# Operands of w2 that are raw blocks, the k chunks of turned heads, and who issues the copies

## The chip, the cores and the metric

One kernel runs on one core of a Trainium2 chip. Its time is the device time of one execution in microseconds (us), as the median of several executions; one further execution was profiled. Names used below: PE is TensorE (PEld its weight loads), DVE VectorE, ACT ScalarE, POOL GpSimd, SP SyncE. SP issues most transfers (DMAs), ACT some.

## The reference, cut to what matters

Two stages. A linear attention with decay gives x of 3072 tokens x 512; then four experts, each a product with w1, a relu and a product with w2, are summed with the tokens' gates.

```python
q, k, v: (4, 8, 768, 64); lam: (8,); w1: (4, 512, 1024); w2: (4, 1024, 512)
def _attn_ref(q, k, v, lam):
    for b in range(nb):                      # blocks of 64 tokens
        intra = np.einsum('bhic,bhjc->bhij', qb, kb) * Dmask[None]
        intra = np.einsum('bhij,bhjd->bhid', intra, vb)
        inter = np.einsum('bhid,bhde->bhie', qb * lam_pow[None], kv_state)
        out[:, :, sl] = intra + inter
        kb_dec = kb * rev_pow[None]
        kv_state = lam_block[None, :, None, None] * kv_state + np.einsum('bhsd,bhse->bhde', kb_dec, vb)
def _moe_ref(x, domain_probs, w1, w2):
    p = domain_probs / (domain_probs.sum(-1, keepdims=True) + 1e-09)
    for e in range(E):
        h = np.maximum(x @ w1[e], 0.0)
        out += p[:, e:e + 1] * (h @ w2[e])
```

## The kernel before

*Units.* The 3072 tokens are three groups of 1024, and a unit is a group g with an expert e: 12 units in the order (0; 0,1,2,3), (1; 1,2,3,0), (2; 2,3,0,1), so unit 5 is group 1 with expert 2, unit 7 group 1 with expert 0, and unit 11, FINAL, group 2 with expert 1. While the second product (with w2) of one unit runs on PE, the first product (with w1) of the next unit is interleaved with it, matmul group by matmul group.

*Products.* Every product is done by a scheme of 7 products of half-size blocks in place of 8, M1 to M7, the first product and from unit 5 on (NEST) the second product by two levels of it, the outer M and the inner M. The weights' side of outer product M is one of A11, A12, A22 (a raw block of the weight matrix) or S1 to S4 (a sum: S1 = A21 + A22, S2 = S1 - A11, S3 = A11 - A21, S4 = A12 - S2), by the table A_OF: M1 A11, M2 A12, M3 S4, M4 A22, M5 S1, M6 S2, M7 S3. Inside, the same table is applied to the quarters of that block, so that each outer product needs seven 128x256 operands: three raw quarters (A11, A12, A22) and four sums. The order of outer products in a unit is SEQ3 = M1, M3, M5, M7, M6, M2, M4; inner ones go in the order INNER = M1, M7, M6, M4, M5, M2, M3.

*Who makes the operands.* For w2 of each expert `prepare_w2_ops` lists steps ("chores"): load blocks of w2 into tiles w2b, form the outer sums w2o on POOL (`total`), and for each outer M form the four inner sums ops on POOL (`ready`, `inner_w2`) and store all seven operands to w_ops, that is w2_ops[e, M] in the chip's memory, 896 KB for one M. Later `feed3` loads them back in four transfers w2t (two operands of 128x256 at a time, the fourth one operand), or, for FINAL, in one transfer of all seven into a tile w2s that stays. `feed3` first calls `until(("w2", expert, M))`, which issues whatever chores and stores still stand ahead of that M, all at once.

*When they are issued.* The order of all instructions is fixed when the program is built. The loop at the end walks over units, outer products and 8 slots each; after each slot `pump` takes stores that are due and perhaps one chore from a list. Whether a chore is begun hangs on a planner's estimates: `busy` (POOL's work), `moved` (the transfer engines' work) and `asked` (SP's issues), of which the last two are raised by the helper `send` (L110 to L114) and compared with the slot now in `pump`. Transfers that a line issues by `dma_start` itself don't raise them. POOL and SP each go through their own list in order, and an instruction waits for what it needs, with all behind it on its engine.

*Attention of groups 1 and 2* runs in between, a chunk n of 128 tokens at a time (n = 8 to 23). `load` brings q and k in two transfers each, by r, the halves of the heads (h = 4r + i); the tile holds heads in the order i, r. `decayed` multiplies k by its decay on POOL. For chunks from 13 on (`comes_across`) q and k also come turned by another way: `bring_across` makes 128 small copies of q and k into a buffer `across`, issued by `trickle` one at a time: on SP, or on ACT where the argument says so, in unit 0's odd slots. `load_across` reads them.

*Lines for what follows.* L117 all POOL and DVE sums; L114 all transfers through `send`; L1148 PE, inner products of the first product; L1514 PE, inner products of the second product from unit 5 on; L1165 ACT relu of the first product's results, whose output m POOL multiplies with decay (m<-m,decay, the gates).

Of the kernel before, what the change touches and what calls it, by code (L numbers as in the profile page):

```python
# [12 lines left out]
ALU = mybir.AluOpType  # L13
# [8 lines left out]
def kernel(  # L22
# [30 lines left out]
    nc = tc.nc  # L53
# [38 lines left out]
    def small(name):  # L92
        return pool.tile([P, W], FP32, name=name, tag="t")
# [66 lines left out]
    def load(n, names="qkv"):  # L160

        c, b = where(n)
        for name in names:
            x = ({"k": acc_tile, "v": w2_tile} if n < CPG else {}).get(name, small)(f"{name}n")
            src = {"q": q, "k": k, "v": v}[name][b, :, c * C:(c + 1) * C, :]
            if name == "v":
                to, of = x[:].rearrange("p (h d) -> p h d", d=D), src.rearrange("h p d -> p h d")
                for h in (slice(0, 4), slice(4, 8)) if n < CPG else (slice(0, 8),):
                    send(out=to[:, h], in_=of[:, h], by=nc.scalar if n == 0 and h.start else None)
            else:  # L170
                to, of = x[:].rearrange("p (i r d) -> p i r d", r=2, d=D), src.rearrange("(r i) p d -> p i r d", r=2)
                for r in range(2):
                    by = nc.scalar if n == 0 and r == 1 else nc.sync
                    by.dma_start(out=to[:, :, r], in_=of[:, :, r])  # L174
            nat[n, name] = x[:].rearrange("p (h d) -> p h d", d=D)


# [15 lines left out]
    def store(f):  # L193
        queue.append((busy[0] + (8 if spare else 2), f))
# [125 lines left out]


    INNER = ("M1", "M7", "M6", "M4", "M5", "M2", "M3")

    def inner_w2(e, m, blk, two):
        b = {f"A{i + 1}{j + 1}": blk[j][:, :, i * P:(i + 1) * P] for i in range(2) for j in range(2)}
        s = [x.rearrange("p c d -> p (c d)").rearrange("p (k c d) -> p k c d", k=2, c=2) for x in two("ops")]
        for name, x, y, op in S_OPS:
            b[name] = s[SLOT[name] // 2][:, SLOT[name] % 2]
            tt(nc.gpsimd, b[name], b[x], b[y], op)
        to = w2_ops[e, MS.index(m)]  # L330
        b["S3"] = s[0]
        at = (("A11", 0), ("S3", slice(1, 3)), ("A22", 3), ("S1", 4), ("A12", 5), ("S4", 6))
        store(lambda: ([send(out=to[:, x], in_=b[n]) for n, x in at], made.add(("w2", e, m))))

    def prepare_w2_ops(e, eased):
        st = {}

        def two(name):
            if eased:
                t = [small(name)[:] for _ in range(2)]  # L340
            else:
                t = stage.tile([P, 2, W], FP32, name=name, tag="st")
                t = [t[:, q] for q in range(2)]
            return [x.rearrange("p (c d) -> p c d", c=2) for x in t]

        def block(name, i, j):
            t = st[name] = two("w2b")
            for q in range(2):
                r = j * W + q * 256
                src = moe_w2[e, r:r + 256, i * DH:(i + 1) * DH]  # L350
                send(out=t[q], in_=src.rearrange("(c p) d -> p c d", p=P))

        def total(name, a, b, op):
            t = two("w2o")
            for q in range(2):
                tt(nc.gpsimd, t[q], st[a][q], st[b][q], op)
            st[name] = t

        def ready(m):
            inner_w2(e, m, st[A_OF[m]], two)  # L360

        if not eased:
            return weight_steps(block, total, ready)

        def less():
            a, b = st["A11"], st.pop("A21")
            for q in range(2):
                tt(nc.gpsimd, b[q], a[q], b[q], ALU.subtract)
            st["S3"] = b

        def drop(*names):
            for n in names:
                del st[n]

        return [
            lambda: (block("A21", 1, 0), block("A22", 1, 1)), pause(6),
            lambda: total("S1", "A21", "A22", ALU.add),
            lambda: (ready("M4"), block("A11", 0, 0), drop("A22")), pause(4),
            less, lambda: ready("M7"), lambda: (ready("M1"), drop("S3")), lambda: ready("M5"),
            lambda: (total("S2", "S1", "A11", ALU.subtract), block("A12", 0, 1)), lambda: ready("M6"),  # L380
            lambda: ready("M2"),
            lambda: total("S4", "A12", "S2", ALU.subtract), lambda: ready("M3"),
        ]

# [272 lines left out]
    def decayed(n):  # L657

        kn = nat[n, "k"]
        kd = kn if n >= CPG else small("kd")[:].rearrange("p (h d) -> p h d", d=D)  # L660
        nat[n, "kd"] = kd
        by = k_decay.rearrange("p r ac -> p ac r").unsqueeze(3).to_broadcast([P, NHP, 2, D])
        tt(nc.gpsimd, *(x.rearrange("p (ac r) d -> p ac r d", r=2) for x in (kd, kn)), by, ALU.mult)

    carried = set()

# [20 lines left out]
    def turn(n, tags):  # L687
        all_added()
        begin_state(n)
        if comes_across(n):  # L690
            turn_across(n)
            return
        if n < CPG:
            decayed(n)
        qn, kn = nat.pop((n, "q")), nat[n, "k"]
        qp = bank(tags[0], "qp")
        kp = bank(tags[1], "kp")
        for x, y in ((qp, qn), (kp, kn)):
            for ac in range(NHP):
                nc.tensor.transpose(  # L700
                    out=x[:, ac * C:(ac + 1) * C], in_=y[:, 2 * ac:2 * ac + 2].rearrange("p r d -> p (r d)"),
                    identity=ident[:],
                )
        if n >= CPG:
            decayed(n)
        del nat[n, "k"]
        qT, kT = small("qT"), small("kT")
        nc.scalar.copy(out=qT[:], in_=qp[:])
        nc.scalar.copy(out=kT[:], in_=kp[:])
        if n >= CPG:  # L710
            turned[n] = qT, kT, qT
            return
        qs = small("qs")
        scaled = lambda: scale_q(qs, qp)
        soon(n, scaled)
        turned[n] = qT, kT, qs, scaled

    def scores(n, tags):
# [19 lines left out]
        for ac in range(NHP):  # L738
            for x in range(1 if last else 2):
                for r in range(2):  # L740
                    nc.tensor.matmul(  # L741
                        out=sp[x][half[r], 256 + ac * D:256 + (ac + 1) * D], lhsT=kd[half[x], 2 * ac + r],
                        rhs=vn[half[x], 4 * r + ac], start=False, stop=True, skip_group_check=True,
                    )
        st = small("st")
# [503 lines left out]
    def feed3(e, m, k):  # L1249

        x_e = units[e][1]
        until(("w2", x_e, m))
        if e == FINAL and m != SEQ3[0]:

            if k == 0:
                t = xp.tile([P, 7, 256], FP32, name="w2s", tag="x" + SEQ[SEQ3.index(m)])
                if (e, m) == PLAIN:
                    i, j = int(A_OF[m][1]) - 1, int(A_OF[m][2]) - 1
                    src = moe_w2[x_e, j * W:(j + 1) * W, i * DH:(i + 1) * DH]
                    send(out=t[:, 0:4], in_=src.rearrange("(k p) d -> p k d", p=P))  # L1260
                    fed3[e, m, 0] = t
                    return
                send(out=t[:], in_=w2_ops[x_e, MS.index(m)].rearrange("p k c d -> p k (c d)"))
                for x in range(4):
                    fed3[e, m, x] = t[:, 2 * x:min(2 * x + 2, 7)]
            return
        t = w2pool.tile([P, 2, DH], FP32, name="w2t", tag="w2")
        n = min(2, 7 - 2 * k)
        send(
            out=t[:, 0:n], in_=w2_ops[x_e, MS.index(m), :, 2 * k:2 * k + n].rearrange("p k c d -> p k (c d)"),  # L1270
        )
        fed3[e, m, k] = t

# [218 lines left out]
    def nested_product(e, m, tags):  # L1494
# [8 lines left out]

        def inner(x, i):
            if (e, m) == END and i in ("M2", "M3"):
                turned_product(("M2", "M3").index(i), b[B_OF[i]], fed3[e, m, x // 2][:, x % 2])
                return
            t = tags[0] if i in ("M1", "M6", "M5", "M3") else tags[1]
            fresh = i in ("M1", "M7", "M2")
# [2 lines left out]
            p = banks[t]  # L1512
            for c in range(2):
                nc.tensor.matmul(  # L1514
                    out=p[:, 0:256], lhsT=fed3[e, m, x // 2][:, x % 2, c * P:(c + 1) * P],
                    rhs=b[B_OF[i]][:, c * 256:(c + 1) * 256], start=(fresh and c == 0), stop=True,
                    skip_group_check=True,
                )
# [295 lines left out]
    for at, (g, e) in enumerate(units):  # L1814
# [14 lines left out]
        for i in range(7):  # L1829
# [41 lines left out]
            for x, part in enumerate(order):  # L1871
# [52 lines left out]
                while steps and (at * 7 + i) * 8 + x == steps[0][0]:  # L1924
                    steps.pop(0)[1]()
                if at == 0 or x % 2 or at == 1 and x == 4:
                    trickle(1, nc.scalar if at == 0 and x % 2 else None)
                for h in range(1, NG):
                    if x == 3 and 0 <= at * 7 + i - FILL[h] < 7:
                        x_fill(h, SEQ[at * 7 + i - FILL[h]])  # L1930
# [31 lines left out]
```

## Time and profile before

| | us |
|---|---|
| median of 3 runs | 1143.09 (1141.39 to 1143.7) |
| profiled execution, its own time | 1141.95 |
| its span, from the first to the last instruction | 1140.2 |
| PE busy | 1130.8 (7991 matmuls) |
| DVE, POOL, ACT busy | 771.7, 767.7, 381.1 |
| PE busy, 0 to 50 us | 44.38 of 50 |
| PE busy, 370 to 500 us | 130.00 of 130 |
| PE busy, 1090 to 1141 us | 46.83 of 51 |
| transfers: loads of w_ops for the second product, issues | 172 (129 of 256 KB, 43 of 128 KB) |
| transfers: stores of those operands, issues | 168 (28 of 256 KB, 140 of 128 KB) |

The profiled execution stands 1.14 us below the median of the runs. A line of a timeline gives the start, the time to the end of the group, engine, line, operation, output tile<-input tiles, shapes and how many there are; in square brackets stands the idle time of the engine before it and what ended it. Groups of transfers give their size and the median time from issue to landing. The granted clock (PEclk) is 1.00 in every stretch up to 1090 us and 0.98 in the last one.

### The profile page before, as it was taken

Reading aid. Unit: us, or ns where it says so; the run is one execution under the profiler, and the core shown is the slowest. Engines: PE = TensorE matmul, PEld = TensorE weight load, DVE = VectorE, ACT = ScalarE, POOL = GpSimd, SP = SyncE. Lnnn points to the kernel's source line nnn. Section 1 sums busy time; section 2 is a strip of 40 time slices with the busy share of each in tenths; the row PEclk is TensorE's granted clock in tenths of the full one; section 3 lists DMA queues with packets and bytes.
Section 4 is the critical chain, followed back from the end, with each engine's and each line's share of the span. In section 5 each row is a group of like instructions: output and inputs, shape, how many; then the busy total and the mean of one; then the engine's idle time right before and its main releaser. Section 6 shows DMA issues by size and latency. Waiting matters only on the chain.

```text
span 1140.2 us, 22167 instructions
## 1 busy us (share of the span) xinstructions
PE 1130.8 (99%) x7991; PEld 987.7 (87%) x7991; DVE 771.7 (68%) x1472; ACT 381.1 (33%) x770; POOL 767.7 (67%) x734
## 2 busy tenths in 40 slices
PE   8999999999999999999999999999999999999998
PEld 7788888888888888888888888888888888888887
DVE  4576775588577757837655566878767576776785
ACT  4325123212312321232343442444354452342332
POOL 2747148655852984854884997995995873873885
PEclk9999999999999999999999999999999999999999
DMA  8796889899989999987867669976779757657553
GB/s 195 173 281 183 214 226 265 276 299 279 310 270 323 301 311 303 312 279 233 260 204 249 200 182 286 347 241 199 223 235 277 217 161 213 189 159 214 168 194 74
DMA packets 321436, 271.58 MB, mean 238 GB/s; under 512 B 150640, under 2 KB 256304, under 8 KB 321328
## 3 DMA queue, kind: packets, MB, share of 16 engines
q1 hardware_dynamic: 298528, 264.37, 76.1%
q10 hardware_dynamic: 22768, 5.80, 2.5%
q8 instruction: 64, 1.05, 0.4%
q14 instruction: 44, 0.36, 0.1%
q0 software_dynamic: 32, 0.00, 0.0%
HBM read 197.19 MB, written 78.68 MB: 242 GB/s over the span
## 4 chain that ended last, share of the span: by engine, by line
PE 97%; SPq 1%; DMA 1%; DVE 0%; issue 0%; ACT 0%; DVEq 0%
PE pg L1148 41%; PE pq L1514 25%; PE q L1207 21%; PE pM L1656 2%; PE pc L1656 2%; PE op L797 1%; PE sp L734 1%; PE op L815 1%; PE sp L741 1%; DMA qn<-in_q_dram 1%; SPq L114 1%; PE pM L1381 1%; PE pg L1514 1%; SPq L174 0%; PE qp L700 0%; PE kp L700 0%
## 5 line engine op out<-in xcount | busy, mean ns | idle before, releaser
L1148 PE MATMUL pg<-xs,ws_in 128*128 128x256 f32 x1960 | 470.2, 380 | 0.4 <-DVE m L117 0.4
L1148 PEld LDWEIGHTS pg<-xs,ws_in 128*128 128x128 f32 x1960 | 371.0, 190 | 53.5 <-DVE m L117 3.2
L117 DVE TENSOR_TENSOR m<-pg,m 128x512 f32<-128x512 f32 x374 | 255.4, 686 | 91.7 <-PE pg L1148 81.4
L1207 PE MATMUL q<-w2t,m 128*128 128x256 f32 x1120 | 265.6, 380 | 0.0
L1207 PEld LDWEIGHTS q<-w2t,m 128*128 128x128 f32 x1120 | 211.7, 190 | 29.3 <-issue 0.3
L117 DVE TENSOR_TENSOR sums<-pq,sums 128x256 f32<-128x256 f32 x272 | 113.1, 421 | 90.6 <-PE pq L1514 78.4
L117 POOL TENSOR_TENSOR m<-m,decay 128x512 f32<-128x512 f32 x91 | 114.5, 1271 | 82.4 <-ACT m L1165 65.4
L1514 PE MATMUL pq<-acc,w2t 128*128 128x256 f32 x688 | 169.2, 379 | 0.0
L1514 PEld LDWEIGHTS pq<-acc,w2t 128*128 128x128 f32 x688 | 130.5, 190 | 18.0
L1165 ACT ACTIVATE m<-m 128x512 f32<-128x512 f32 x99 | 62.4, 630 | 190.9 <-DVE m L117 186.7
L1225 DVE SCALAR_TENSOR_TENSOR acc<-q,gate,acc 128x256 f32<-128x256 f32 x108 | 52.0, 482 | 75.6 <-PE q L1207 74.8
L117 DVE TENSOR_TENSOR m<-m,m 128x512 f32<-128x512 f32 x108 | 96.6, 894 | 6.5 <-ACT m L1131 6.5
L1161 ACT COPY m<-pg 128x512 f32<-128x512 f32 x88 | 51.5, 586 | 121.6 <-PE pg L1148 114.2
L117 POOL TENSOR_TENSOR acc<-hT,hT 128x512 f32<-128x512 f32 x56 | 70.3, 1270 | 21.7 <-PE pq L1514 13.9
L1125 ACT COPY pg<-m 128x512 f32<-128x512 f32 x77 | 45.5, 591 | 110.2 <-DVE m L117 108.1
L117 POOL TENSOR_TENSOR acc<-hT,acc 128x512 f32<-128x512 f32 x56 | 71.2, 1272 | 7.0 <-PE pq L1514 3.2
L1514 PE MATMUL pq<-hT,w2t 128*128 128x256 f32 x288 | 70.0, 379 | 0.0
L117 POOL TENSOR_TENSOR w2o<-w2b 128x512 f32<-128x512 f32 x26 | 36.7, 1437 | 45.6 <-DMA w2b<-in_moe_w_dram 39.3
L1514 PEld LDWEIGHTS pq<-hT,w2t 128*128 128x128 f32 x288 | 54.7, 190 | 7.4
L117 POOL TENSOR_TENSOR kn<-kn,decay 128x512 f32<-128x512 f32 x16 | 19.1, 1197 | 55.9 <-PE kp L700 29.8
L1129 ACT COPY m<-pg 128x512 f32<-128x512 f32 x44 | 25.7, 585 | 91.8 <-PE pg L1148 91.8
L1514 PE MATMUL pq<-m,w2t 128*128 128x256 f32 x228 | 55.4, 379 | 0.0
(157 smaller groups left out, 1453.3 us busy)
## 6 DMA issues: line engine op xcount, KB each, us to landing
w2t<-w_ops SPq DMA_DIRECT2D x129, 256.0 KB, 3.3
ws_in<-w_ops SPq DMA_DIRECT2D x40, 512.0 KB, 4.7
ws_in<-w_ops SPq DMA_DIRECT2D x60, 256.0 KB, 4.0
ws_in<-w_ops SPq DMA_DIRECT2D x40, 384.0 KB, 4.3
w2b<-in_moe_w_dram SPq DMA_DIRECT2D x56, 256.0 KB, 4.9
w_ops<-ops SPq DMA_DIRECT2D x28, 512.0 KB, 4.7
w2t<-w_sums SPq DMA_DIRECT2D x40, 256.0 KB, 4.7
w_sums<-w2o SPq DMA_DIRECT2D x16, 512.0 KB, 5.4
```

The costliest lines, as they stand in the source:

```text
L114: (by or nc.sync).dma_start(out=out, in_=in_)
L117: eng.tensor_tensor(out=o, in0=a, in1=b, op=op)
L734: nc.tensor.matmul(out=sp[r][half[x], ac * BL:(ac + 1) * BL], lhsT=hc(kT)[half[r], ac, blk[x]], rhs=hc(qT)[half[r], ac, blk[x]], start=(ac ...
L1125: nc.scalar.copy(out=banks[tags[1]][:], in_=new["11"][:])
L1129: nc.scalar.copy(out=o[:], in_=p[:])
L1148: nc.tensor.matmul(out=p[:, j * 256:(j + 1) * 256], lhsT=ws[i][:, j * P:(j + 1) * P], rhs=xs[i], start=(fresh and j == 0), stop=True, skip ...
L1161: nc.scalar.copy(out=new[at][:], in_=p[:])
L1165: nc.scalar.activation(out=new[at][:], in_=new[at][:], func=AF.Relu)
L1207: nc.tensor.matmul(out=p[:, s * DH:(s + 1) * DH], lhsT=h[A_OF[m]][:, c * 256 + s * P:c * 256 + (s + 1) * P], rhs=fed2[g, e, m][uu][:, c], ...
L1225: nc.vector.scalar_tensor_tensor(out=o, in0=x, scalar=w, in1=o, op0=ALU.mult, op1=ALU.add)
L1514: nc.tensor.matmul(out=p[:, 0:256], lhsT=fed3[e, m, x // 2][:, x % 2, c * P:(c + 1) * P], rhs=b[B_OF[i]][:, c * 256:(c + 1) * 256], start= ...
L1656: nc.tensor.matmul(out=p[:, s * 256:(s + 1) * 256], lhsT=a[c][:, f:f + P], rhs=b[:, c, j * 256:(j + 1) * 256], start=(s == 0 and c == 0 an ...
```

## The change

- `load`: for chunks that come across, k is loaded in one transfer with heads in the order r, i, where there were two, and through `send`. `decayed` and the matmuls that use k are told of the other order.
- `inner_w2`: for outer products of a raw block (M1, M2, M4) only the four sums are stored; for those of a sum all seven, grouped so that fewer transfers are needed (the two sum tiles as 256 KB each; A12 and A22 together where they lie together).
- tiles of w2's blocks are read as (i, c, d) or (c, i, d) as they were loaded; the outer sums are written with i outside.
- `feed3`: raw quarters of M1, M2 and M4 are read from w2 itself (`raw_w2`), the rest from w2_ops; the operands are looked up by inner product. FINAL's M2 (PLAIN) needs no operands, and they are no longer prepared.
- `trickle`: ACT issues the copies in odd slots of all units, not of unit 0 alone.

```diff
--- before.py
+++ after.py
@@ -169,9 +169,15 @@
                     send(out=to[:, h], in_=of[:, h], by=nc.scalar if n == 0 and h.start else None)
             else:
                 to, of = x[:].rearrange("p (i r d) -> p i r d", r=2, d=D), src.rearrange("(r i) p d -> p i r d", r=2)
-                for r in range(2):
-                    by = nc.scalar if n == 0 and r == 1 else nc.sync
-                    by.dma_start(out=to[:, :, r], in_=of[:, :, r])
+                if comes_across(n):
+                    to = x[:].rearrange("p (r i d) -> p i r d", r=2, d=D)
+                    send(out=x[:].rearrange("p (h d) -> p h d", d=D), in_=src.rearrange("h p d -> p h d"))
+                else:
+                    for r in range(2):
+                        by = nc.scalar if n == 0 and r == 1 else nc.sync
+                        by.dma_start(out=to[:, :, r], in_=of[:, :, r])
+                nat[n, name] = to
+                continue
             nat[n, name] = x[:].rearrange("p (h d) -> p h d", d=D)
 
 
@@ -320,17 +326,32 @@
 
 
     INNER = ("M1", "M7", "M6", "M4", "M5", "M2", "M3")
+    OPS_AT = {"A11": 0, "S3": 1, "S2": 2, "S1": 3, "S4": 4, "A12": 5, "A22": 6}
+
+    def raw_w2(e, m, name):
+        (i, j), (x, y) = ((int(n[1]) - 1, int(n[2]) - 1) for n in (A_OF[m], name))
+        r, d = j * W + y * 256, i * DH + x * P
+        return moe_w2[e, r:r + 256, d:d + P].rearrange("(c p) d -> p c d", p=P)
 
     def inner_w2(e, m, blk, two):
-        b = {f"A{i + 1}{j + 1}": blk[j][:, :, i * P:(i + 1) * P] for i in range(2) for j in range(2)}
-        s = [x.rearrange("p c d -> p (c d)").rearrange("p (k c d) -> p k c d", k=2, c=2) for x in two("ops")]
+        b = {f"A{i + 1}{j + 1}": blk[j][:, :, i] for i in range(2) for j in range(2)}
+        of = two("ops")
+        s = [x.rearrange("p (k c d) -> p k c d", k=2, c=2) for x in of]
         for name, x, y, op in S_OPS:
             b[name] = s[SLOT[name] // 2][:, SLOT[name] % 2]
             tt(nc.gpsimd, b[name], b[x], b[y], op)
         to = w2_ops[e, MS.index(m)]
-        b["S3"] = s[0]
-        at = (("A11", 0), ("S3", slice(1, 3)), ("A22", 3), ("S1", 4), ("A12", 5), ("S4", 6))
-        store(lambda: ([send(out=to[:, x], in_=b[n]) for n, x in at], made.add(("w2", e, m))))
+        pieces = [(to[:, 1 + 2 * x:3 + 2 * x], s[x]) for x in range(2)]
+        if A_OF[m][0] == "S":
+            pieces += [(to[:, 0], b["A11"])]
+            if together(blk[1]):
+                pieces += [(to[:, 5:7], blk[1].rearrange("p c i d -> p i c d"))]
+            else:
+                pieces += [(to[:, OPS_AT[n]], b[n]) for n in ("A12", "A22")]
+        store(lambda: ([send(out=x, in_=y) for x, y in pieces], made.add(("w2", e, m))))
+
+    def together(x):
+        return packet(x.rearrange("p c i d -> p i c d")) == W
 
     def prepare_w2_ops(e, eased):
         st = {}
@@ -341,17 +362,21 @@
             else:
                 t = stage.tile([P, 2, W], FP32, name=name, tag="st")
                 t = [t[:, q] for q in range(2)]
-            return [x.rearrange("p (c d) -> p c d", c=2) for x in t]
+            return t
+
+        def as_loaded(t):
+            return [x.rearrange("p (c i d) -> p c i d", c=2, i=2) for x in t]
 
         def block(name, i, j):
-            t = st[name] = two("w2b")
+            t = two("w2b")
+            st[name] = as_loaded(t)
             for q in range(2):
                 r = j * W + q * 256
                 src = moe_w2[e, r:r + 256, i * DH:(i + 1) * DH]
-                send(out=t[q], in_=src.rearrange("(c p) d -> p c d", p=P))
+                send(out=t[q].rearrange("p (c d) -> p c d", c=2), in_=src.rearrange("(c p) d -> p c d", p=P))
 
         def total(name, a, b, op):
-            t = two("w2o")
+            t = [x.rearrange("p (i c d) -> p c i d", c=2, i=2) for x in two("w2o")]
             for q in range(2):
                 tt(nc.gpsimd, t[q], st[a][q], st[b][q], op)
             st[name] = t
@@ -378,7 +403,7 @@
             lambda: (ready("M4"), block("A11", 0, 0), drop("A22")), pause(4),
             less, lambda: ready("M7"), lambda: (ready("M1"), drop("S3")), lambda: ready("M5"),
             lambda: (total("S2", "S1", "A11", ALU.subtract), block("A12", 0, 1)), lambda: ready("M6"),
-            lambda: ready("M2"),
+            *([lambda: ready("M2")] if e != units[FINAL][1] else []),
             lambda: total("S4", "A12", "S2", ALU.subtract), lambda: ready("M3"),
         ]
 
@@ -657,10 +682,12 @@
     def decayed(n):
 
         kn = nat[n, "k"]
-        kd = kn if n >= CPG else small("kd")[:].rearrange("p (h d) -> p h d", d=D)
+        kd = kn if n >= CPG else small("kd")[:].rearrange("p (i r d) -> p i r d", r=2, d=D)
         nat[n, "kd"] = kd
         by = k_decay.rearrange("p r ac -> p ac r").unsqueeze(3).to_broadcast([P, NHP, 2, D])
-        tt(nc.gpsimd, *(x.rearrange("p (ac r) d -> p ac r d", r=2) for x in (kd, kn)), by, ALU.mult)
+        if comes_across(n):
+            kd, kn, by = (x.rearrange("p i r d -> p r i d") for x in (kd, kn, by))
+        tt(nc.gpsimd, kd, kn, by, ALU.mult)
 
     carried = set()
 
@@ -698,7 +725,7 @@
         for x, y in ((qp, qn), (kp, kn)):
             for ac in range(NHP):
                 nc.tensor.transpose(
-                    out=x[:, ac * C:(ac + 1) * C], in_=y[:, 2 * ac:2 * ac + 2].rearrange("p r d -> p (r d)"),
+                    out=x[:, ac * C:(ac + 1) * C], in_=y[:, ac].rearrange("p r d -> p (r d)"),
                     identity=ident[:],
                 )
         if n >= CPG:
@@ -739,7 +766,7 @@
             for x in range(1 if last else 2):
                 for r in range(2):
                     nc.tensor.matmul(
-                        out=sp[x][half[r], 256 + ac * D:256 + (ac + 1) * D], lhsT=kd[half[x], 2 * ac + r],
+                        out=sp[x][half[r], 256 + ac * D:256 + (ac + 1) * D], lhsT=kd[half[x], ac, r],
                         rhs=vn[half[x], 4 * r + ac], start=False, stop=True, skip_group_check=True,
                     )
         st = small("st")
@@ -1249,7 +1276,9 @@
     def feed3(e, m, k):
 
         x_e = units[e][1]
-        until(("w2", x_e, m))
+        ops, ready = w2_ops[x_e, MS.index(m)].rearrange("p k c d -> p k (c d)"), A_OF[m][0] == "S"
+        if (e, m) != PLAIN:
+            until(("w2", x_e, m))
         if e == FINAL and m != SEQ3[0]:
 
             if k == 0:
@@ -1260,16 +1289,24 @@
                     send(out=t[:, 0:4], in_=src.rearrange("(k p) d -> p k d", p=P))
                     fed3[e, m, 0] = t
                     return
-                send(out=t[:], in_=w2_ops[x_e, MS.index(m)].rearrange("p k c d -> p k (c d)"))
-                for x in range(4):
-                    fed3[e, m, x] = t[:, 2 * x:min(2 * x + 2, 7)]
+                if ready:
+                    send(out=t[:], in_=ops)
+                else:
+                    send(out=t[:, 1:5], in_=ops[:, 1:5])
+                    for n in ("A11", "A22", "A12"):
+                        send(out=t[:, OPS_AT[n]].rearrange("p (c d) -> p c d", c=2), in_=raw_w2(x_e, m, n))
+                fed3.update({(e, m, i): t[:, OPS_AT[A_OF[i]]] for i in INNER})
             return
         t = w2pool.tile([P, 2, DH], FP32, name="w2t", tag="w2")
-        n = min(2, 7 - 2 * k)
-        send(
-            out=t[:, 0:n], in_=w2_ops[x_e, MS.index(m), :, 2 * k:2 * k + n].rearrange("p k c d -> p k (c d)"),
-        )
-        fed3[e, m, k] = t
+        names = [A_OF[i] for i in INNER[2 * k:2 * k + 2]]
+        fed3.update({(e, m, i): t[:, x] for x, i in enumerate(INNER[2 * k:2 * k + 2])})
+        stored = [n for n in names if ready or n[0] == "S"]
+        for n in names:
+            if n not in stored:
+                send(out=t[:, names.index(n)].rearrange("p (c d) -> p c d", c=2), in_=raw_w2(x_e, m, n))
+        x, y = OPS_AT[stored[0]], OPS_AT[stored[-1]]
+        at = names.index(stored[0])
+        send(out=t[:, at:at + len(stored)], in_=ops[:, x:y + 1:max(y - x, 1)])
 
 
 
@@ -1503,7 +1540,7 @@
 
         def inner(x, i):
             if (e, m) == END and i in ("M2", "M3"):
-                turned_product(("M2", "M3").index(i), b[B_OF[i]], fed3[e, m, x // 2][:, x % 2])
+                turned_product(("M2", "M3").index(i), b[B_OF[i]], fed3[e, m, i])
                 return
             t = tags[0] if i in ("M1", "M6", "M5", "M3") else tags[1]
             fresh = i in ("M1", "M7", "M2")
@@ -1512,7 +1549,7 @@
             p = banks[t]
             for c in range(2):
                 nc.tensor.matmul(
-                    out=p[:, 0:256], lhsT=fed3[e, m, x // 2][:, x % 2, c * P:(c + 1) * P],
+                    out=p[:, 0:256], lhsT=fed3[e, m, i][:, c * P:(c + 1) * P],
                     rhs=b[B_OF[i]][:, c * 256:(c + 1) * 256], start=(fresh and c == 0), stop=True,
                     skip_group_check=True,
                 )
@@ -1924,7 +1961,7 @@
                 while steps and (at * 7 + i) * 8 + x == steps[0][0]:
                     steps.pop(0)[1]()
                 if at == 0 or x % 2 or at == 1 and x == 4:
-                    trickle(1, nc.scalar if at == 0 and x % 2 else None)
+                    trickle(1, nc.scalar if x % 2 else None)
                 for h in range(1, NG):
                     if x == 3 and 0 <= at * 7 + i - FILL[h] < 7:
                         x_fill(h, SEQ[at * 7 + i - FILL[h]])
```

## The prediction

> **What bounds the kernel now.** I read the page's busy times and chain first, then the table of stretches, and then the timelines of POOL, SP and PE around the one place where the new order of work bites.
>
> ```profile
> PE 1130.8 (99%) x7991; PEld 987.7 (87%) x7991; DVE 771.7 (68%) x1472; ACT 381.1 (33%) x770; POOL 767.7 (67%) x734
> PE 97%; SPq 1%; DMA 1%; DVE 0%; issue 0%; ACT 0%; DVEq 0%
> ```
>
> The chain that ended last is PE for 97% of the span: TensorE is the bound. The stretches say where it is not:
>
> ```profile
> core 0: us, PE busy (x) PEld busy (x) DVE busy (x) ACT busy (x) POOL busy (x), PEclk, DMA share, GB/s
> 50.00:255.00 205.00, 205.00 (x1674) 179.55 (x1674) 138.84 (x260) 56.92 (x122) 116.99 (x118) 1.00 0.86 244
> 255.00:370.00 115.00, 114.56 (x1104) 99.86 (x1103) 83.92 (x161) 25.71 (x58) 60.48 (x63) 1.00 0.96 297
> 711.00:764.00 53.00, 53.00 (x245) 46.20 (x245) 42.31 (x86) 23.35 (x42) 49.57 (x44) 1.00 0.93 298
> 764.00:1090.00 326.00, 326.00 (x1510) 286.35 (x1509) 230.24 (x429) 129.87 (x243) 231.40 (x196) 1.00 0.68 207
> ```
>
> After 50 us PE has no gap to speak of: matmuls of 128x256 start 216 ns apart at a granted clock of 1.00, and start to start their excess over that pace adds up to about 1 us until 1090 us (0.6 of it at 343 us). The first 50 us, where PE idles, keep their instruction order; the first new place in SP's order lies near 190 us. So whatever the change relieves, it can gain about 1 us. A loss has no such ceiling, and the row of 711 to 764 us shows where it can come from: POOL is busy 49.57 of 53 us.
>
> **The change, part by part.**
>
> *k of turned chunks in one transfer:* 22 issues on SP become 11; the same 256-byte runs. An issue holds SP for 0.43 us (median), so 4.7 us of SP. SP is off PE's path: 0. But these loads now go through the helper that adds to the planner's estimates of transfer and issue time, so the planner starts chores at other moments. That shift, not the transfer, is what I price below.
>
> *ACT issues copies in odd steps of all units:* 39 issues move from SP to ACT (13, 13, 12 and 1 by stretches of unit, 194 to 326 us): SP −16.8 us, ACT +39 x 0.56 = 21.8 us, spread over 132 us in which ACT is about a quarter busy (25.71 of 115). What is queued behind such an issue are ACT's copies into and out of PSUM, for which DVE and PE wait. The 28 copies that ACT issues already, at 91 to 192 us, hold it 0.56 to 0.69 us each, its longest wait before one is 1.3 us, and PE stands at its floor beside them. PE's matmuls that follow an ACT copy have 0.8 us or more of slack. Bounds: 0 to 39 x 0.1 = 4 us if one issue in eight exposed 0.8 us; nearest row is the 28 without a loss, so 0.
>
> *Raw blocks of w2's operands aren't stored:* stores of operands 168 to 89, loads 172 to 229 (raw blocks come straight from w2 in 512-byte runs), the last unit's resident operands of one product in 4 transfers instead of 1; with k and the copies SP issues 69 fewer (−30 us). POOL loses 4 subtractions (M2's operands of the last unit's expert, 3 us); its sums S2 and S4 are written permuted, priced as the rows of 128x512 (1.27 to 1.44 us). DMA is no bound (share 0.68 to 0.96, PE full). Gain: 0 to 1 us, taken 0.
>
> *What moves with it.* The instructions of PE and DVE keep their order. POOL's and SP's chores do not, between 190 and 765 us. I laid the new order of POOL and SP over the old times of PE, ACT and DVE with the durations of the old rows. Two places come out short.
>
> *Place B, unit 7 (token group 1, expert 0), second matrix product's M3, used by PE at 763.8 us.* Before, on POOL, on SP and on PE:
>
> ```profile
> start us, us, engine line op out<-in xcount [idle before <-releaser]
> 711.77 1.27 POOL L117 TENSOR_TENSOR m<-m,decay 128x512 f32<-128x512 f32 x1 [5.81 <-ACT m L1165]
> 715.47 2.50 POOL L117 TENSOR_TENSOR w2o<-w2b,w2o 128x512 f32<-128x512 f32 x2
> 723.09 1.41 POOL L117 TENSOR_TENSOR ops<-w2o 128x256 f32<-128x256 f32 x2
> 725.38 0.73 POOL L117 TENSOR_TENSOR ops<-w2o,ops 128x256 f32<-128x256 f32 x1
> ```
>
> ```profile
> 740.31 0.32 SPq L114 DMA_DIRECT2D w_ops<-ops  x1
> 749.25 4.71 SPq L114 DMA_DIRECT2D w2t<-w_ops  x3
> ```
>
> ```profile
> 763.80 1.03 PE L1514 MATMUL pq<-m,w2t 128*128 128x256 f32 x4
> ```
>
> POOL has S4 at 715.5 and M3's operands at 726.1; the last store issues at 740.3 and lands at 743.3, the load at 749.25 lands at 752.7: 11.1 us in hand. In the new order, as the built program lists it, expert 0's sums are behind: when M3's first load is due they are not made, so `until(("w2", 0, "M3"))` issues all the rest there. From the same release at 711.77 (ACT's m) POOL has 47 instructions up to M3's last operand:
> - 23 of 128x512 (11 m<-m,decay, 12 acc) x 1.27 = 29.2 us
> - 4 w2o x 1.27 to 1.44 = 5.1 to 5.8 us
> - 20 ops of 128x256 x 0.745 = 14.9 us
>
> That is 49.2 to 49.9 us, and each one's inputs are there before its turn: the end is at 761.0 to 761.7. M3's first load (A11 and S3) waits for the piece of A11, the third of four stores, SP issuing it about 0.8 us later, 761.8 to 762.5. The landing:
>
> ```profile
> w2t<-w_ops SPq DMA_DIRECT2D x129, 256.0 KB, 3.3
> w_ops<-w2o SPq DMA_DIRECT2D x39, 128.0 KB, 3.9
> ```
>
> Store 3.0 (smallest near there) to 4.2, so 764.8 to 766.7; the load issues then, behind the store and four w2b loads of the next expert, and lands 3.3 to 3.8 later: 768.1 to 770.5. Against 763.8 PE stands 4.3 to 6.7 us; I take 5.8, from POOL's later end and medians of 3.9 and 3.5 (761.9 + 0.4 + 3.9 + 3.4 = 769.6). What is late next: M3's other loads (3.1 and 2.1 us short by themselves) are issued 0.4 us apart behind the first and are needed 3.5 us and more after it, so the shift covers them. PE's order is fixed, so nothing else runs meanwhile, and with no idle after it the whole span moves.
>
> The Trainium skill ("DMA: Bandwidth & Descriptors", Anatomy of one DMA) says a transfer costs about 2.0 us fixed, mostly the receipt of the write, plus bytes at 436 KB per us. By that estimate the 128 KB store is 2.3 us and the 256 KB load 2.6, and the sum would be 1145.8. No row of this trace comes so low for these two, and the stretch has the DMA engines 93% busy, so the rows stay.
>
> *Place A, unit 3's M1, operands used at 291.7 to 296.0 us.* Before, these loads land 3.0 to 4.8 us early. In the new order the subtractions ops<-w1b of that expert stand on POOL behind the decay of a chunk's k (lands 273 to 275) and four block sums: done 279.8 to 282. Store of 512 KB +3.9 to 4.9, load +3.1 to 4.4: 287 to 291.4, the raw part up to 294. Stall 0 to 3.5 us, taken 0.7, since the two ends meet the need (292.5 and 296.0) only at the slow ones.
>
> Elsewhere the new order leaves every load in time; the tightest are the accumulators at 752.6 to 768.1 (0.9 to 1.6 us in hand).
>
> *Sum, on the profiled execution's own time:* 1141.95 (span 1140.2 and 1.75 around it) + 5.8 + 0.7 = 1148.5. The median of the runs is 1143.09, 1.1 above that execution; halfway is 1149.0, my forecast.
>
> **Rivals.**
> 1. *Both places cost in full.* For it: at 255 to 370 us DMA is 0.96 busy, and landings lengthen there. 1141.95 + 6.7 + 3.5 = 1152.2. Against: the medians just meet the need.
> 2. *ACT's copies get in the way.* An issue on ACT that waits for an earlier transfer holds PSUM copies; 4 us more at the bound above: 1152.5. Against: the 28 old ones.
> 3. *Not slower: POOL catches up before M3.* It decides at one point: the load is in time if M3's last operand is done by 763.8 − 3.3 − 3.9 − 1.0 = 755.6 us, 5.4 us or more before my sum. Then nothing is late and the time is 1141 to 1142.5 (up to 1 us gained). For it: POOL was idle 5.81 us before 711.77, which chores could fill. Against: in the new order the chores are not issued there, and 47 instructions in 43.8 us would need 0.93 us each where the rows give 1.05.
>
> **How the numbers follow.** The forecast has 0.67, rival 1 has 0.15, rival 2 0.08, rival 3 0.10. 0.2% (2.3 us) is what a measurement of this kernel can tell from no change. Faster by that needs twice what PE idles after 50 us: 0.03, which leaves 0.07 of rival 3 for no change; slower 0.90. The range: 1141.95 + 4.3 − 1 = 1145.2 below, reaching a little towards rival 3, so 1144.8; above, both places in full with the median's 1.1 and 1 us: 1154.5.
>
> **What would show it.** Right: a gap of PE of 4 to 7 us before the first matmul of unit 7's M3, ended by a w2t load from w_ops, with POOL working without a gap from 711 to 761 us; the stretches behind it of the same length as before; fewer SP issues with no effect on PE. Place A: a gap below 3.5 us near 292 us on ws_in. Wrong: no gap at M3 (rival 3); gaps on ACT between 194 and 326 us (rival 2); a gap at a load from raw w2, which would mean that 512-byte runs land later than I took.

## The result

The changed kernel takes 1149.88 us (median of 6, 1148.14 to 1151.26), the kernel before 1143.39 us (median of 6 of the same series): ratio 1.0056, interval 1.0041 to 1.007. That is slower, 0.9 us from the forecast of 1149.0. The profiled execution took 1149.36 us with a span of 1147.6, against 1140.2 before: 7.4 us more.

The page's first lines and chain of the changed kernel:

```profile
PE 1134.2 (99%) x7991; PEld 990.9 (86%) x7991; DVE 765.9 (67%) x1472; ACT 381.4 (33%) x770; POOL 762.9 (66%) x730
PE 97%; DVE 1%; DMA 1%; issue 0%; ACT 0%; SPq 0%; DVEq 0%; POOLq 0%; ACTq 0%
```

The same number of PE instructions is busy 3.4 us longer, so some of them ran slower; and nothing in these shares tells that a wait was added. The view of waits of PE tells it, as a single wait of the second product for a load of w2's operands:

```profile
PE pq L1551 <- DMA w2t<-w_ops: 5.2, 1, 5.2
```

The stretches around it, from the table of windows (columns as in the prediction):

```profile
700.00:755.00 55.00, 54.94 (x254) 47.91 (x254) 43.52 (x86) 22.01 (x40) 43.07 (x42) 1.00 0.83 265
762.00:768.20 6.20, 1.18 (x6) 0.70 (x4) 1.60 (x4) 1.66 (x3) 6.04 (x6) 0.93 0.94 282
768.20:775.00 6.80, 6.60 (x18) 5.36 (x19) 2.04 (x4) 0.59 (x1) 5.09 (x5) 0.56 1.08 365
775.00:790.00 15.00, 15.00 (x71) 13.22 (x70) 11.38 (x25) 7.07 (x13) 8.66 (x8) 1.00 0.59 180
```

PE stands until 768.4 us. Then it is busy, but at a granted clock of 0.56: 18 matmuls in 6.6 us where 31 fit at full pace. From 775 us on the clock is 1.00. PE's timeline shows both parts:

```profile
761.29 1.89 PE L1175 MATMUL pg<-xs,ws_in 128*128 128x256 f32 x8
768.40 2.04 PE L1551 MATMUL pq<-m,w2t 128*128 128x256 f32 x4 [5.23 <-DMA w2t<-w_ops]
770.24 1.91 PE L1551 MATMUL pq<-acc,w2t 128*128 128x256 f32 x4
771.95 2.99 PE L1175 MATMUL pg<-xs,ws_in 128*128 128x256 f32 x8
```

Four matmuls take 1.9 to 2.0 us here; the same four took 1.03 at 763.80 us before. Counted from the start of one matmul to the start of the next, the gap costs 5.4 us and the slow matmuls 2.9 us. Everything else of the trace gave back 0.9.

What is late is the chain that the prediction named. POOL's timeline, from the release at 711 us to M3's last operand:

```profile
710.91 1.27 POOL L117 TENSOR_TENSOR m<-m,decay 128x512 f32<-128x512 f32 x1 [11.47 <-ACT m L1192]
736.23 8.63 POOL L117 TENSOR_TENSOR m<-m,decay 128x512 f32<-128x512 f32 x7
754.23 2.50 POOL L117 TENSOR_TENSOR w2o<-w2b,w2o 128x512 f32<-128x512 f32 x2
758.98 0.72 POOL L117 TENSOR_TENSOR ops<-w2o,ops 128x256 f32<-128x256 f32 x1
```

and SP's, with M3's stores, the next expert's four loads and M3's own first loads:

```profile
748.98 11.07 SPq L114 DMA_DIRECT2D w_ops<-ops  x4
760.10 0.95 SPq L114 DMA_DIRECT2D w_ops<-w2o  x2
761.10 2.04 SPq L114 DMA_DIRECT2D w2b<-in_moe_w_dram  x4
763.23 1.40 SPq L114 DMA_DIRECT2D w2t<-w_ops  x3
```

POOL has no idle time between the first and the last of its lines. The operands that were done at 726.1 us before are done at 759.7.

### The profile page after: what moved, and what is told of

It is laid out like the page before. It is cut to its first block, busy times and chain, and to the rows that moved or that the text cites. A ratio compares the mean times of both kernels' runs of the same rounds, so it can differ in the third digit from the quotient of the medians.

```text
span 1147.6 us, 22118 instructions
## 1 busy us (share of the span) xinstructions
PE 1134.2 (99%) x7991; PEld 990.9 (86%) x7991; DVE 765.9 (67%) x1472; ACT 381.4 (33%) x770; POOL 762.9 (66%) x730
## 4 chain that ended last, share of the span: by engine, by line
PE 97%; DVE 1%; DMA 1%; issue 0%; ACT 0%; SPq 0%; DVEq 0%; POOLq 0%; ACTq 0%
PE pg L1175 41%; PE pq L1551 25%; PE q L1234 21%; PE pM L1693 2%; PE pc L1693 2%; PE op L824 1%; PE sp L761 1%; PE op L842 1%; PE sp L768 1%; PE pM L1418 1%; PE pg L1551 1%; PE qp L727 1%; PE kp L727 0%; DMA w2t<-w_ops 0%; DMA decay<-in_lam_dram 0%
## 5 line engine op out<-in xcount | busy, mean ns | idle before, releaser
L1252 DVE SCALAR_TENSOR_TENSOR acc<-q,gate,acc 128x256 f32<-128x256 f32 x108 | 52.1, 483 | 80.5 <-PE q L1234 79.7
L117 DVE TENSOR_TENSOR m<-m,m 128x512 f32<-128x512 f32 x108 | 88.0, 815 | 6.5 <-ACT m L1158 6.5
L117 POOL TENSOR_TENSOR kn<-kn,decay 128x512 f32<-128x512 f32 x16 | 18.4, 1148 | 65.2 <-DMA kn<-in_k_dram 31.3
L117 POOL TENSOR_TENSOR w2o<-w2b 128x512 f32<-128x512 f32 x26 | 33.7, 1319 | 41.2 <-DMA w2b<-in_moe_w_dram 36.6
```

The source lines that it names most:

```text
L117: eng.tensor_tensor(out=o, in0=a, in1=b, op=op)
L1252: nc.vector.scalar_tensor_tensor(out=o, in0=x, scalar=w, in1=o, op0=ALU.mult, op1=ALU.add)
```

## The experiments

Each was compared with the kernel before in runs on the same chip, in three series of four (medians of before 1145.07, 1145.57 and 1146.10 us; rows 1 to 4, 5 to 8 and 9 to 12). The intervals are 95%.

| run | median us | ratio to before | interval |
|---|---|---|---|
| the whole change, k not counted | 1142.04 | 0.9970 | 0.9956 to 0.9983 |
| raw blocks and ACT's copies | 1142.40 | 0.9979 | 0.9965 to 0.9993 |
| k alone | 1165.02 | 1.0176 | 1.0148 to 1.0203 |
| before, k only counted | 1166.24 | 1.0183 | 1.0160 to 1.0205 |
| the change again | 1149.90 | 1.0041 | 1.0025 to 1.0057 |
| gap filled, 40 matmuls | 1151.99 | 1.0056 | 1.0040 to 1.0073 |
| w2b behind | 1144.61 | 0.9991 | 0.9980 to 1.0003 |
| raw blocks alone | 1145.04 | 1.0001 | 0.9983 to 1.0019 |
| gap filled, 20 matmuls | 1150.93 | 1.0039 | 1.0022 to 1.0056 |
| ACT's copies alone | 1143.08 | 0.9980 | 0.9967 to 0.9992 |
| k not counted, alone | 1143.94 | 0.9983 | 0.9970 to 0.9997 |
| the whole change, k not counted, again | 1141.79 | 0.9966 | 0.9955 to 0.9977 |

### Is it the estimates or the transfers?

The changed kernel with one line of it altered:

```diff
-                    send(out=x[:].rearrange("p (h d) -> p h d", d=D), in_=src.rearrange("h p d -> p h d"))
+                    nc.sync.dma_start(out=x[:].rearrange("p (h d) -> p h d", d=D), in_=src.rearrange("h p d -> p h d"))
```

> The change in full, but k of the turned chunks is issued by dma_start itself in its one transfer, so that it doesn't raise the planner's estimates of transfer and issue time. Theory (the loss comes from the chores that these estimates put off, and nothing else): no gap of PE before unit 7's M3 at 763 us, time of the kernel before within 1.5 us, 1142 to 1144.5. Rival (the transfers themselves cost it: raw blocks that land late, or ACT's issues): the gap stays and the time is that of the change, 1149 to 1151.

No wait of PE near 763 us is left, and the loss is gone; the kernel is even 0.3% faster than before, 3.0 us, where a difference of up to 1.5 was expected. Its stretch there:

```profile
755.00:775.00 20.00, 20.00 (x94) 17.62 (x93) 15.35 (x33) 9.83 (x18) 18.26 (x17) 1.00 0.66 206
```

The mirror of it: the kernel before, with the two transfers of k as they were, but counted.

```diff
-                    by.dma_start(out=to[:, :, r], in_=of[:, :, r])
+                    (send if comes_across(n) else by.dma_start)(out=to[:, :, r], in_=of[:, :, r])
```

> The kernel before with one edit: k of the turned chunks, still in two transfers, goes through the helper that raises the planner's estimates. No transfer changes; only the order of chores does. Theory: as k alone, a gap of about 10.4 us at unit 7's M3 and half clock behind it, 1154 to 1159. Rival (the form of the transfer matters, not the estimates): the time of the kernel before, 1142 to 1144.5.

No transfer changed its form, and the kernel lost 1.8%. Its waits and PE's gap:

```profile
PE pq L1514 <- DMA w2t<-w_ops: 11.1, 2, 10.8
PE pg L1148 <- DVE m L117: 5.3, 2, 4.4
```

```profile
250.00:400.00 150.00, 143.85 (x1399) 124.58 (x1401) 102.51 (x195) 33.64 (x75) 72.72 (x79) 0.98 0.92 280
771.00:785.00 14.00, 4.83 (x23) 3.90 (x21) 5.17 (x11) 3.25 (x6) 13.61 (x14) 0.77 0.79 241
785.00:795.00 10.00, 8.38 (x27) 6.97 (x28) 2.70 (x6) 1.66 (x3) 7.40 (x7) 0.65 0.99 348
```

The gap (10.8 us) and the slow stretch behind it (clock 0.65) came out as expected, 13.7 us start to start. The time is 7 us above the upper end of the expectation, since the new order also makes PE wait between 250 and 400 us (143.85 of 150 us busy, where the kernel before had 149.56) and then work at half clock there for some us behind the longest of these waits, 4.4 us: 8.5 us start to start, which laying the order over old times had not shown. k alone (the hunks of load, decayed, turn and scores on the kernel before), with its one transfer counted, does the same:

> k in one transfer alone. Theory: the chores are put off further than in the whole change, since here all pieces of w2's operands must still be stored: laying the new order over the old times, M3's first load is 11.7 us late (the same sum said 6.7 for the whole change, where 5.4 was measured), so a gap of about 10.4 us, and some 3 us behind it in which PE's granted clock is about half: 1143.4 + 13.4 = 1157, from 1154 to 1159. Rival (one transfer of k in place of two is harmless by itself, and the loss needs the raw blocks): 1142 to 1144.5.

Measured 1165.02 us, above the range too, with a gap of 11.1 us at M3 and a wait of 2.5 us for ws_in and 2.6 us for DVE's m earlier. So the planner's estimates put the chores off, and the form of the transfer has no part in the loss. Without k, the two other parts (the changed kernel with the hunks of load, decayed, turn and scores taken back):

> Two of the three parts without k: raw blocks not stored and ACT issuing copies in odd steps of all units; k in two transfers as before. Theory: both parts are off the path that sets the end, no gap at 763 us, 1142 to 1144.5; SP issues 58 fewer and it is worth under 1 us. Rival (raw blocks read in 512-byte runs land late, or ACT's copies come late): 1147 or more, with gaps of PE ended by w2t from w2 or by ACT.

1142.40 us: no gap at M3, and the rival falls: reading raw blocks in 512-byte runs isn't late here. The kernel is 2.7 us faster than the kernel before, where under 1 us was expected.

### What makes up the gap?

The changed kernel, in which the step that forces out M3's stores begins no further chore, so that the next expert's loads w2b come later:

```diff
     def until(what):
         while what not in made:
-            pump(force=True)
+            pump(force=True, still=what if what == ("w2", 0, "M3") else None)
...
-        if begins:
+        if begins and still not in made:
```

> The changed kernel with one move on SP: the four loads of the next expert's blocks (w2b) that stood between the last stores of expert 0's M3 and M3's first load are put 11 transfers later. Theory (SP's four issues hold the load 1.1 us past the landing of the store, and the w2b transfers stretch it from 3.3 to 5.0 us): the load issues at about 762.2 and lands at 765.5 to 766.5, the gap shrinks from 5.4 to 2.7 to 3.7 us, and the half clock behind it may shrink too: 2 to 5 us less than the changed kernel. Rival (the landing of the store or POOL alone sets the load): gap 4.5 us or more, under 1 us gained.

The gap shrinks to 1.9 us, more than expected, and the time is that of the kernel before. PE's timeline, the stretch behind the gap, and SP's timeline:

```profile
767.15 1.10 PE L1551 MATMUL pq<-m,w2t 128*128 128x256 f32 x4 [1.87 <-DMA w2t<-w_ops]
768.09 1.03 PE L1551 MATMUL pq<-acc,w2t 128*128 128x256 f32 x4
```

```profile
768.00:775.00 7.00, 7.00 (x35) 6.15 (x34) 4.25 (x9) 3.15 (x6) 6.84 (x7) 1.00 0.99 314
```

```profile
762.21 0.95 SPq L114 DMA_DIRECT2D w_ops<-w2o  x2
764.31 1.56 SPq L114 DMA_DIRECT2D w2t<-w_ops  x3
```

The store of A11 was issued at 762.21 and landed at 764.24; the load went out 0.07 us later and landed 2.7 us after its issue, and PE started on it at 767.15. In the changed kernel A11's store landed at 762.13, but SP was issuing w2b loads until 763.14, and M3's load, behind 1 MB of them, took 5.0 us (763.23 to 768.27). So of the 5.4 us, 1.1 was SP's queue and 2.3 the transfers ahead of it; the 2.0 that are left are POOL's and the store's. With a gap of 1.9 us the clock stayed at 1.00: the first four matmuls behind it take 1.10 us, the next four 1.03. Against the changed kernel's second measurement, below, the median is 5.3 us lower, about what the shorter gap (3.2) and the full clock (1.8) come to in the traces.

### Is the slow clock a cost of its own?

The changed kernel once more, as the measure:

> The changed kernel itself, as the measure for the next two on the same chip. Expected 1149 to 1151 against 1143 to 1145 of the kernel before: gap of 5.4 us at unit 7's M3 and about 3 us of half clock behind it.

It repeats: 1149.90 us, a gap of 5.1 us, and behind it, in this execution, 1.8 us of slow matmuls instead of 2.9. The granted clock tells why the two differ. It stands at 0.50 from 767.3 to 774.2 us in the first profiled execution and from 769.0 to 772.4 us in this one:

```profile
767.40:774.00 6.60, 5.60 (x13) 4.54 (x14) 2.04 (x4) 0.06 (x1) 4.89 (x5) 0.50 1.06 360
769.10:772.30 3.20, 3.20 (x9) 2.53 (x8) 0.42 (x1) 0.00 (x0) 3.04 (x3) 0.50 1.09 362
```

PE works for 5.8 us of the one stretch and 3.6 us of the other, and loses half of that. The stretches are 6.8 and 3.4 us long, and in all traces of these runs, up to 1090 us, half clock comes in stretches of about 3.4, 6.8 or 13.7 us only. A gap need not be as long as 5 us for it: in k alone PE waited 2.5 us, up to 270.85 us, and the clock stood at half in the next 3.4 us.

```profile
267.90:271.30 3.40, 0.91 (x5) 0.51 (x4) 1.32 (x3) 0.63 (x1) 0.00 (x0) 1.00 1.08 326
271.40:274.60 3.20, 3.20 (x87) 2.55 (x89) 1.29 (x2) 1.34 (x4) 0.00 (x0) 0.50 0.79 183
```

Then PE was kept busy in the gap of the changed kernel:

```diff
+            for _ in range(40 if (units[e], m, i) == ((1, 0), "M3", "M1") else 0):
+                nc.tensor.matmul(out=p[:, 0:P], lhsT=ident[:], rhs=ident[:], start=True, stop=True)
```

> The changed kernel with 40 matmuls of 128x128 of the identity added on PE just before the matmul that waits in unit 7's M3; their result is overwritten. At 0.11 us each they fill some 4.3 of the 5.4 us. Theory (the half clock behind the gap follows from PE standing idle, and is a cost of its own beside the wait): the wait for the load stays, the granted clock stays 1.00 behind it, and the time is 2.5 to 3 us less than the changed kernel's, though work was added: about 1147. Rival (the slow matmuls behind the gap are due to something else, such as the transfers at 365 GB/s in that stretch): the same time as the changed kernel within 0.7 us, and PE still at half pace.

This missed (1151.99 us, some 1147 expected) by its size: each added matmul became two instructions, and the 80 of them ran more than 2 us past the landing of the load.

```profile
764.47 9.09 PE L1551 MATMUL pq<-ident 128*128 128x128 f32 x80
773.40 1.03 PE L1553 MATMUL pq<-m,w2t 128*128 128x256 f32 x4
```

```profile
768.00:775.00 7.00, 7.00 (x58) 6.82 (x58) 0.42 (x1) 0.00 (x0) 5.76 (x5) 1.00 1.06 357
```

But the added matmuls, and M3's behind them, run at full pace, with the transfers at 357 GB/s in that stretch, so it isn't the transfers that slow PE. The same with 20:

> As the run with the gap filled, with 20 added matmuls in place of 40: each of them took two PE instructions of 0.11 us, so that 40 ran for 8.9 us and past the load's landing. 20 run for 4.4 us and end before it. Theory (half clock follows from idleness): the wait ends with the load, some 0.7 us are left of the gap, the clock stays 1.00, and the time is that of the changed kernel less what the half clock costs, 1.7 to 3 us: 1147 to 1148. Rival: as the changed kernel, 1149.5 to 1150.5, with PE at half pace behind the load.

```profile
767.40 4.63 PE L1551 MATMUL pq<-ident 128*128 128x128 f32 x40
772.44 1.13 PE L1553 MATMUL pq<-m,w2t 128*128 128x256 f32 x4 [0.41 <-DMA w2t<-w_ops]
773.41 1.03 PE L1553 MATMUL pq<-acc,w2t 128*128 128x256 f32 x4
```

In the trace the half clock is gone: the fill and the rest of the wait cost 5.0 us together, with a clock of 1.00 behind them, where gap and slow matmuls cost 8.3 and 7.0 us in the two executions without a fill. The time doesn't show it (1150.93 us where 1147 to 1148 was expected; its ten executions spread from 1146.68 to 1155.13, so that 1.8 to 2.9 us can't be told). The profiled execution, 1151.66 us, had lost its time elsewhere: PE reached this place 3.6 us later than in the kernel before, and 2.8 of these were lost in the first 52 us. That idleness causes the half clock is shown by the traces of these runs; that filling it pays is not shown.

### Where do the 3 us of gain come from?

> Raw blocks of w2's operands not stored, alone. The two parts without k were 0.2% faster than the kernel before, which a prediction from one profiled execution had put at 0 to 1 us. Theory (fewer and fewer bytes of transfers, 271.6 to 266 MB, shorten the small waits between 250 and 500 us, where the transfer engines are 0.96 to 0.98 busy): raw blocks alone give most of it, ratio 0.997 to 0.9995. Rival (SP is relieved by ACT's issues, and that gives it): ratio 0.9995 to 1.001 here.

Ratio 1.0001: not storing the raw blocks gives nothing that can be measured, and the theory of fewer bytes falls. (Edit: only the hunks of w2's operands.) The two others alone, `trickle`'s condition and k in one transfer by `dma_start`:

> ACT issues the copies in odd steps of all units, alone. Raw blocks alone gave a ratio of 1.0001 to the kernel before, raw blocks with ACT's copies 0.9979, the three with k uncounted 0.9970. Theory (SP's issues come sooner in 190 to 330 us when ACT takes 39 of them, so fewer loads are a little late): ratio 0.997 to 0.9995. Rival (ACT's issues do harm or nothing by themselves; the gain needs raw blocks as well): 0.9995 to 1.002.

> k of the turned chunks in one transfer, not counted by the planner, alone. Theory (only the estimates made k's part cost anything): no gap at unit 7's M3, ratio 0.998 to 1.0005. Rival (one transfer of k in place of two is late for itself): gaps ended by kn, 1.002 or more.

0.9980 and 0.9983, both below 1 and both where they were expected. And all three together again:

> The whole change with k uncounted once more, beside its parts on the same chip: 0.996 to 0.9985 of the kernel before, if the first result holds; 0.9995 or more, if it was the luck of that chip.

0.9966, so the 0.3% holds in a second series, and of the versions run this is the one that beats both kernels most clearly. Two parts that take issues from SP (39 and 11) each give some 0.2%. That the relief of SP is what gives it is not shown: which waits they shorten wasn't settled, since no single wait that is gone from their traces is in the profile of before. The kept traces, one execution each, say little more. After 50 us, raw blocks alone has a wait of 1.1 us of PE for ws_in at 266 us, and k not counted, alone, one of 1.3 us at 265 us and one of 1.2 at 367 us; the whole change with k not counted has none above 0.2 us in either of its two traces. And PE's 1101st instruction starts at 52.1 us in the kernel before but between 50.3 and 54.8 us in the traces of the runs, though SP's order there is the same in all of them: a good part of the spread arises before anything was changed.

## Why the prediction was right, and where it was not

- *The place and the chain* (place B: S4 and M3's operands made late, the load behind the store, PE standing at M3): right, and shown from both sides, by taking away its cause in the changed kernel and putting it into the kernel before. The cause, k's loads counted by the planner, was right too.
- *POOL's 47 instructions, 49.2 to 49.9 us from the release:* measured 48.8, from a release 0.9 us earlier; the end was at 759.7 instead of 761.0 to 761.7.
- *The store, 3.0 to 4.2 us:* too long; A11's store landed after 2.0 us. Here the Trainium skill's estimate that the prediction set aside ("DMA: Bandwidth & Descriptors", Anatomy of one DMA; 2.3 us for 128 KB, from a fit for DMAs issued from GpSimd, where SP issues these) was nearer than the median of the rows. That no row came so low holds for medians only: single transfers of the kernel before took 1.8 us and more (128 KB stores of operands) and 2.5 us and more (256 KB loads w2t).
- *The load, 3.3 to 3.8 us after issue:* too short; 5.0 us behind four w2b loads, and 2.7 us without them. The same estimate, 2.6 us, is near the second and has no term for the first. SP's four issues, in the prediction's words "behind the store and four w2b loads", were the later release by 1.1 us, not the store; the sum has no term for them. The errors cancel, which is luck: 5.4 us of gap against 5.8 taken. The sum itself is not quite the lines above it, which end POOL at 761.7 and not 761.9, give SP about 0.8 us and not 0.4, and a median of 3.5 and not 3.4: with these it is 6.1 us. And with the Trainium skill's two figures in place of its own the sum gives 3.4 us at M3 and a time of 1146.6, not 1145.8.
- *"With no idle after it the whole span moves":* the failed part of this step. The span moved by more, because PE's clock fell to half for 6.8 us in one execution and 3.4 in another: 2.9 and 1.8 us. The prediction had no such term. The Trainium skill ("TensorE: Matmul & The Clock Gate", HAM oscillation) has as its rule that PE should have no idle gaps of more than about 3.4 us. The gaps of 5.2 us (half clock) and 1.9 us (none) agree with it, the one of 2.5 us in k alone (half clock) does not, so that the limit here lies lower.
- *Place A, 0.7 us taken:* it cost nothing. k landed some 3 us sooner than over the old times, so POOL had the operands ready at 278.5, the store landed at 283.0 (forecast 284 to 287) and the load at 285.6, used at 291.5 us: 5.9 us early.
- *ACT's copies, 0; raw blocks, 0; k's transfer, 0; "it can gain about 1 us":* a mis-sized term. (Of the 28 old issues on ACT, read as 0.56 to 0.69 us each, one took 1.2.) The three together without the counting gain 0.30 and 0.34%, 3.4 to 3.9 us. The bound of 1 us was read from one profiled execution of 1141.95 us, and that is among the quickest: over the three series the kernel before ran from 1140.35 to 1150.26 us with medians of 1145 to 1146. A wait that strikes some executions only need not be in the page of a quick one. That this is where the gain lies is likely but not shown, and whether it is as large in the series of the result, where the kernel before has a median of 1143.39 us, wasn't run.
- *The sum:* 5.8 + 0.7 = 6.5 us was forecast on the profiled execution. In its place stand about 5.4 for the gap, 1.8 to 2.9 for the clock and minus 3.4 to 3.9 for the relief: 3.3 to 4.9 us. On the median of 1145.57 of the series in which the change was run again that makes 1148.9 to 1150.5, and 1149.90 was measured there, 4.3 us above the kernel before; in the series of the result the difference was 6.5. That the time came out within 0.9 us is partly luck: two terms that were missing have opposite signs.
- *The rivals:* both places in full, ACT in the way and POOL catching up are each refuted: no wait at 292 us, ACT's copies alone 0.9980, POOL without idle from 711 us on.

## What to carry to other kernels

Where a planner issues work by estimates, sending one more transfer through the helper that counts it can move the whole order: compare the order on each engine, and lay it over the old times, before pricing the transfer itself. A gap of PE is to be priced with the slow matmuls behind it (here from 2.5 us on, not at 1.9 us), and a load that is late should not stand behind a megabyte of loads that nobody waits for yet. Read the spread of the runs beside the profile: a quick profiled execution can hide what relief is worth in the ordinary ones.

## What the runs showed of the hardware

A matmul of 128x128 in f32 became two PE instructions of 0.11 us each (80 instructions in 9.09 us for 40). A 256 KB load landed 2.7 us after its issue on a queue with little ahead and 5.0 us with 1 MB of loads issued in the 2 us before it. Behind a gap of 5.1 to 5.2 us PE's matmuls started about 0.43 us apart in place of 0.216, for 1.8 us of loss in one execution and 2.9 in another of the same kernel, because the granted clock stood at 0.50 for 3.4 us in the one and 6.8 us in the other; behind a gap of 2.5 us it stood at 0.50 for 3.4 us, and behind 1.9 us it did not fall.
